# One load for two, a release by VectorE, and a split last store in a streaming multiply-add kernel

## The chip, the cores and the metric

The kernel runs on one core of a Trainium2 chip, with the other cores idle. The metric is the device time of one execution in microseconds (us). Each run below also has a profile of one execution, and all executions told of here were marked as in the fast state, with a granted TensorE clock of 1.0. A ratio is the mean time of one kernel's fast runs over that of the other's fast runs of the same rounds on the same chip, so it is not quite the ratio of the medians quoted beside it. The brackets behind a ratio are its 95% interval.

## The reference

```python
B, S, D = 1024, 16, 512          # x, y: [B, S, D] bf16; gamma: [D] bf16
def reference(x, y, gamma):
    return x + gamma * y
```

Seen flat, x and y have 16384 rows of 512 elements, 16.78 MB each. The output is as large, so the kernel moves 50.33 MB.

## The kernel before

Each of the 128 partitions holds 128 rows. The kernel loads y and x, multiplies and adds in place on VectorE, and stores from y's buffer. A partition's rows form three blocks of 4, 60 and 64 rows, each contiguous in DRAM. SyncE issues the loads in one DMA queue (q1 in the profile) and ScalarE issues gamma and the stores in another (q10). All transfers run on the same 16 DMA engines: the two queues' shares of them sum to 98.7%, and at the handover q10's first packets begin one by one as q1's last ones end, from 79.25 to 79.66 us. The trace records them in packets, the pieces that one engine moves one after the other: a load of 64 rows shows as 128 packets of 64 KB, one for each partition, in waves of 16 (the last wave of the changed kernel's loads begins from 77.08 to 77.62), so 8 on every engine.

```python
BLOCKS = [4, 60, 64]
PIECES = [12, 52, 56, 8]          # the pieces that VectorE works on
SP = [
    ('y', 0, 4), ('y', 4, 64),
    ('x', 0, 4, 0), ('x', 4, 64, 4),
    ('y', 64, 128),
    ('x', 64, 120, 12), ('x', 120, 128, 68),   # from row, to row, place in x's buffer
]
ACT = [('g',), ('s', 4, 64), ('s', 0, 4), ('s', 64, 128)]   # gamma, then stores
# ... (how the first loads are held and moved ahead)
RELEASE = ('x', 64, 120, 12)
DVE = [('m', 0), ('m', 1), ('a', 1), ('a', 0), ('m', 2), ('m', 3), ('a', 2), ('a', 3)]
# 'm': y = y * gamma for a piece, 'a': y = x + y for a piece
# ...
    # TensorE waits for the 56-row load of x and lets the stores go
    _take(s_load[RELEASE], 16, nc.tensor)
    nc.tensor.sem_inc(s_go, 1)
    nc.tensor.sem_inc(s_rel, 1)
```

ScalarE waits for `s_go` before its first store. The rows of that store are summed long before, at 58.6 us, so the wait holds the stores back until the loads are nearly through. The last 64 rows of x reuse the part of x's buffer that the first sum frees.

Of the kernel before, what the change touches and what calls it, by code (L numbers as in the profile page):

```python
# [14 lines left out]
    ('x', 0, 4, 0),  # L15
    ('x', 4, 64, 4),
    ('y', 64, 128),
    ('x', 64, 120, 12),
    ('x', 120, 128, 68),
]  # L20
ACT = [('g',), ('s', 4, 64), ('s', 0, 4), ('s', 64, 128)]

EARLY = (2, 0)

HOLD, AHEAD = ('y', 0, 4), (2, 0)

RELEASE = ('x', 64, 120, 12)

DVE = [('m', 0), ('m', 1), ('a', 1), ('a', 0), ('m', 2), ('m', 3), ('a', 2), ('a', 3)]
MULT, ADD = mybir.AluOpType.mult, mybir.AluOpType.add  # L30


def _take(sem, n, eng):


    return eng.wait_ge(sem, n).then_inc(sem, -n)  # L36


def kernel(
# [9 lines left out]
    nc = tc.nc  # L49
# [26 lines left out]
    y_sb = nc.alloc_sbuf_tensor("y_sb", [P, rows, D], dt).ap()  # L76
    x_loads = [w for w in SP + ACT if w[0] == "x"]
    y_loads = [w for w in SP + ACT if w[0] == "y"]
    stores = [w for w in SP + ACT if w[0] == "s"]
    for loads in (x_loads, y_loads, stores):  # L80
# [5 lines left out]
    sem = nc.alloc_semaphore  # L86
    s_gamma, s_ones, s_ps, s_dve = sem("s_gamma"), sem("s_ones"), sem("s_ps"), sem("s_dve")
    s_load = {w: sem("s_" + "_".join(map(str, w[:2]))) for w in x_loads + y_loads}
    s_held = {nc.sync: sem("s_held_sp"), nc.scalar: sem("s_held_act"), nc.vector: sem("s_held_dve")}
    s_add, s_go, s_rel, s_end, s_out = sem("s_add"), sem("s_go"), sem("s_rel"), sem("s_end"), sem("s_out")  # L90
    added = [a for kind, *a in DVE if kind == "a"]
    order = {a[0]: k for k, a in enumerate(added)}

    def meets(a, b, c, d):
        return a < d and c < b
# [4 lines left out]
    def x_at(row):  # L100
        return next(w[3] + row - w[1] for w in x_loads if w[1] <= row < w[2])
# [12 lines left out]
    def ring(eng, what, n_early, n_ahead):  # L114

        known, went = 0, False
        for k, w in enumerate(what):
            kind = w[0]
            if k == n_ahead:
                _take(s_held[eng], 1, eng)  # L120
            need = frees(w) if kind == "x" else pieces_of(w[1], w[2]) + list(w[3:]) if kind == "s" else []
            need = max((order[c] + 1 for c in need), default=0)
            if kind == "s" and not went:
                _take(s_go, 1, eng)
                went = True
            if need > known:
                eng.wait_ge(s_add, need)
                known = need
            if kind == "g":
                i = eng.dma_start(out=gamma_row, in_=gamma.unsqueeze(0)).then_inc(s_gamma, 16)  # L130
            elif kind == "x":
                to = x_sb[:, w[3] : w[3] + w[2] - w[1], :]
                i = eng.dma_start(out=to, in_=rows_of(xf, w[1], w[2])).then_inc(s_load[w], 16)
            elif kind == "y":
                r = slice(w[1], w[2])
                i = eng.dma_start(out=y_sb[:, r, :], in_=rows_of(yf, w[1], w[2])).then_inc(s_load[w], 16)
            else:
                r = slice(w[1], w[2])
                i = eng.dma_start(out=rows_of(of, w[1], w[2]), in_=y_sb[:, r, :]).then_inc(s_out, 16)
            if k < n_early:  # L140
                early.append(i.ins)

    ring(nc.sync, SP, EARLY[0], AHEAD[0])
    ring(nc.scalar, ACT, EARLY[1], AHEAD[1])

# [9 lines left out]
    nc.vector.tensor_copy(out=gamma_sb, in_=gamma_ps).then_inc(s_dve, 1)  # L155
    _take(s_dve, 1, nc.vector)

    _take(s_load[RELEASE], 16, nc.tensor)
    nc.tensor.sem_inc(s_go, 1)
    nc.tensor.sem_inc(s_rel, 1)  # L160

    landed, open_mults = set(), 0

    def need(loads, c):
        for w in loads:
            if w not in landed and meets(starts[c], starts[c + 1], w[1], w[2]):
                if w == RELEASE:
                    _take(s_rel, 1, nc.vector)
                elif w == HOLD:
                    _take(s_held[nc.vector], 1, nc.vector)  # L170
                else:
                    _take(s_load[w], 16, nc.vector)
                landed.add(w)

    for kind, *args in DVE:
        c = args[0]
        yt = y_sb[:, starts[c] : starts[c + 1], :]
        if kind == "m":
            need(y_loads, c)
            g = gamma_sb[:, None, :].to_broadcast([P, PIECES[c], D])  # L180
            nc.vector.tensor_tensor(out=yt, in0=yt, in1=g, op=MULT).then_inc(s_dve, 1)  # L181
            open_mults += 1
        else:
            need(x_loads, c)
            if open_mults:
                _take(s_dve, open_mults, nc.vector)
                open_mults = 0
            at = x_at(starts[c])
            xt = x_sb[:, at : at + PIECES[c], :]
            nc.vector.tensor_tensor(out=yt, in0=xt, in1=yt, op=ADD).then_inc(s_add, 1)  # L190
# [44 lines left out]
```

## Time and profile before

| | before |
|---|---|
| device time, median of 6 runs | 120.03 us (119.81 to 120.50) |
| span of the profiled execution | 118.7 us |
| VectorE busy | 70.0 us, 59% |
| DMA queues q1 and q10, share of 16 engines | 66.0% + 32.7% |
| first store issued | 77.86 us |
| x's last rows landed | 80.0 us |
| last store landed | 118.7 us |

The two DMA shares sum to 98.7%; the prediction works out what follows from that. VectorE is busy for 59% of the span, so what matters in this kernel is whether the DMA engines are ever without a packet, and whether each packet takes its usual time (2.42 us for 64 KB and 2.27 us for 60 KB in these traces). The prediction below looked hard at the first question and hardly at the second.

### The profile page before, as it was taken

How to read it: one execution, taken by the hardware profiler on the slowest of the kernel's cores; microseconds unless marked ns; L12 is line 12 of the kernel's file. 1: busy time of each engine (PE TensorE's matmuls, PEld its weight loads, DVE VectorE, ACT ScalarE, POOL GpSimd, SP SyncE). 2: the span in 40 equal slices, each digit the busy share in tenths (PEclk: the TensorE clock that was granted, in tenths of full speed). 3: DMA queues.
4: the chain of work that ended last, by engine and by line, in shares of the span. 5: the costliest groups of instructions: out<-in, count | busy, mean ns of one | idle time of the engine just before them, and what ended most of it. 6: DMA issues, size and time to landing. Idle time of an engine off the chain costs nothing. (4 is left out here: it accounts for less than half of the span.)

```text
span 118.7 us, 89 instructions
## 1 busy us (share of the span) xinstructions
PE 0.6 (0%) x1; PEld 0.1 (0%) x1; DVE 70.0 (59%) x10; POOL 0.2 (0%) x4
## 2 busy tenths in 40 slices
PE   0001000000000000000000000000000000000000
PEld 0000000000000000000000000000000000000000
DVE  0002000699999299999769999989999910000000
POOL 0000000000000000000000000000000000000000
DMA  9779977999779888988897997897997799988892
GB/s 508 331 332 497 497 331 331 508 414 580 331 331 662 353 353 375 684 353 353 353 618 309 502 425 309 359 635 331 393 600 331 331 403 458 707 353 353 353 596 110
DMA packets 1442, 50.33 MB, mean 424 GB/s; under 512 B 161, under 2 KB 162, under 8 KB 546
## 3 DMA queue, kind: packets, MB, share of 16 engines
q1 hardware_dynamic: 1008, 33.55, 66.0%
q10 hardware_dynamic: 434, 16.78, 32.7%
HBM read 33.56 MB, written 16.78 MB: 424 GB/s over the span
## 5 line engine op out<-in xcount | busy, mean ns | idle before, releaser
L181 DVE TENSOR_TENSOR y_sb<-y_sb,gamma_sb 128x6144 bf16<-128x6144 bf16 (+3 forms) x4 | 34.6, 8689 | 12.3 <-DVEq L36 12.3
L190 DVE TENSOR_TENSOR y_sb<-x_sb,y_sb 128x26624 bf16<-128x26624 bf16 (+3 forms) x4 | 34.6, 8688 | 2.6 <-DVEq L36 2.6
L155 DVE CAST gamma_sb<-gamma_ps 128x512 bf16<-128x512 f32 x1 | 0.7, 692 | 8.6 <-DVEq L36 8.6
L147 DVE MEMSET ones_row<- 1x128 bf16 x1 | 0.2, 165 | 2.0 <-PEq L52 2.0
L153 PE MATMUL gamma_ps<-gamma_row,ones_row 1*128 1x512 bf16 x1 | 0.6, 578 | 10.0 <-PEq L36 10.0
L153 PEld LDWEIGHTS gamma_ps<-gamma_row,ones_row 1*128 1x128 bf16 x1 | 0.1, 99 | 10.0 <-issue 10.0
L219 POOL MEMSET const-bfloat16-1.0<- 128x1 bf16 x1 | 0.1, 102 | 0.0
L219 POOL MEMSET const-uint8-127<- 128x1 uint8 x1 | 0.1, 101 | 0.0
L219 POOL MEMSET const-float32-0.0<- 128x1 f32 x1 | 0.1, 99 | 0.2 <-issue 0.2
L219 POOL MEMSET const-float32-1.0<- 128x1 f32 x1 | 0.1, 98 | 0.0
## 6 DMA issues: line engine op xcount, KB each, us to landing
y_sb<-in_y_dram SPq DMA_DIRECT2D x1, 7680.0 KB, 21.2
x_sb<-in_x_dram SPq DMA_DIRECT2D x1, 7680.0 KB, 37.1
out_dram<-y_sb ACTq DMA_DIRECT2D x1, 7680.0 KB, 20.3
x_sb<-in_x_dram SPq DMA_DIRECT2D x1, 7168.0 KB, 22.2
x_sb<-in_x_dram SPq DMA_DIRECT2D x1, 1024.0 KB, 24.3
y_sb<-in_y_dram SPq DMA_DIRECT2D x1, 512.0 KB, 3.2
x_sb<-in_x_dram SPq DMA_DIRECT2D x1, 512.0 KB, 19.3
out_dram<-y_sb ACTq DMA_DIRECT2D x1, 512.0 KB, 21.1
```

Of the source, the lines that this page charges most:

```text
L147: nc.vector.memset(ones_row, 1.0).then_inc(s_ones, 1)
L153: nc.tensor.matmul(gamma_ps, ones_row, gamma_row, start=True, stop=True).then_inc(s_ps, 1)
L155: nc.vector.tensor_copy(out=gamma_sb, in_=gamma_ps).then_inc(s_dve, 1)
L181: nc.vector.tensor_tensor(out=yt, in0=yt, in1=g, op=MULT).then_inc(s_dve, 1)
L190: nc.vector.tensor_tensor(out=yt, in0=xt, in1=yt, op=ADD).then_inc(s_add, 1)
L219: nc = _bacc.Bacc("TRN2", target_bir_lowering=False, num_devices=1)
```

## The change

The intent was to drop the small load at the end: x's last 64 rows come in one load, the stores are released by an event that falls at about the same time anyway (the end of VectorE's last product), and the last store is split so that the larger part can leave first.

```diff
-    ('x', 64, 120, 12),
-    ('x', 120, 128, 68),
+    ('x', 64, 128, 12),
 ]
-ACT = [('g',), ('s', 4, 64), ('s', 0, 4), ('s', 64, 128)]
+ACT = [('g',), ('s', 4, 64), ('s', 0, 4), ('s', 64, 120), ('s', 120, 128)]
...
-RELEASE = ('x', 64, 120, 12)
-
-DVE = [('m', 0), ('m', 1), ('a', 1), ('a', 0), ('m', 2), ('m', 3), ('a', 2), ('a', 3)]
+DVE = [('m', 0), ('m', 1), ('a', 1), ('a', 0), ('m', 2), ('m', 3), ('go',), ('a', 2), ('a', 3)]
...
-    _take(s_load[RELEASE], 16, nc.tensor)
-    nc.tensor.sem_inc(s_go, 1)
-    nc.tensor.sem_inc(s_rel, 1)
...
+        if kind == "go":
+            _take(s_dve, open_mults, nc.vector)   # the products have ended
+            open_mults = 0
+            nc.vector.sem_inc(s_go, 1)
+            continue
```

More of the change, by code (lines that the diff above doesn't have):

```diff
@@ L89 @@
     s_held = {nc.sync: sem("s_held_sp"), nc.scalar: sem("s_held_act"), nc.vector: sem("s_held_dve")}
-    s_add, s_go, s_rel, s_end, s_out = sem("s_add"), sem("s_go"), sem("s_rel"), sem("s_end"), sem("s_out")
+    s_add, s_go, s_end, s_out = sem("s_add"), sem("s_go"), sem("s_end"), sem("s_out")
     added = [a for kind, *a in DVE if kind == "a"]
@@ L166, in need @@
             if w not in landed and meets(starts[c], starts[c + 1], w[1], w[2]):
-                if w == RELEASE:
-                    _take(s_rel, 1, nc.vector)
-                elif w == HOLD:
+                if w == HOLD:
                     _take(s_held[nc.vector], 1, nc.vector)
```

## The prediction

> **What bounds the kernel now.** I first read the page's busy shares and its DMA queues, because a kernel that multiplies and adds once per element is likely to be bound by its bytes.
>
> ```profile
> PE 0.6 (0%) x1; PEld 0.1 (0%) x1; DVE 70.0 (59%) x10; POOL 0.2 (0%) x4
> ...
> q1 hardware_dynamic: 1008, 33.55, 66.0%
> q10 hardware_dynamic: 434, 16.78, 32.7%
> HBM read 33.56 MB, written 16.78 MB: 424 GB/s over the span
> ```
>
> VectorE works for 59% of the span. The two DMA queues, q1 (all of x and y) and q10 (gamma and the stores), together fill 66.0 + 32.7 = 98.7% of the time of the 16 DMA engines. What is left is 1.3% of 118.7 us, or 1.5 us, and most of it is the start and the final landing. So there is one question: does the change make a hole in the DMA stream, or close one?
>
> Next I asked for windows, in which the last two numbers of a row are the DMA share and the GB/s of packets that began there. A row that starts or ends inside a wave of packets misleads, so I moved the bounds to where one load hands over to the next.
>
> ```profile
> 0.00:0.95 0.95, 0.00 (x0) 0.00 (x0) 0.00 (x0) 0.20 (x4) 1.00 0.00 0
> 0.95:1.40 0.45, 0.00 (x0) 0.00 (x0) 0.00 (x0) 0.00 (x0) 1.00 0.90 146
> ...
> 40.20:59.50 19.30, 0.00 (x0) 0.00 (x0) 17.29 (x2) 0.00 (x0) 1.00 1.00 435
> 59.50:79.24 19.74, 0.00 (x0) 0.00 (x0) 18.38 (x3) 0.00 (x0) 1.00 1.00 423
> 79.24:97.30 18.06, 0.00 (x0) 0.00 (x0) 16.21 (x2) 0.00 (x0) 1.00 1.01 437
> 98.60:118.00 19.40, 0.00 (x0) 0.00 (x0) 0.00 (x0) 0.00 (x0) 1.00 1.00 434
> ```
>
> y's last 64 rows (40.20 to 59.50), the first stores (79.24 to 97.30) and the last store (98.60 to 118.00) all run at 434 to 437 GB/s and a share of 1.00: there are no holes, not even where loads give way to stores. The last 64 rows of x (59.50 to 79.24) run at 423. The share is 1.00 there too, so the engines were busy but moved their packets more slowly: 2.7% of 19.74 us, about 0.5 us by this row.
>
> The timeline gives the order round the handover, and the issue list the times from issue to landing.
>
> ```profile
> 55.31 0.80 SPq L133 DMA_DIRECT2D x_sb<-in_x_dram  x2
> 60.49 17.30 DVE L181 TENSOR_TENSOR y_sb<-y_sb,gamma_sb 128x28672 bf16<-128x28672 bf16 x2 [1.94 <-DVEq L36]
> 77.86 17.96 ACTq L139 DMA_DIRECT2D out_dram<-y_sb  x3
> 78.15 17.29 DVE L190 TENSOR_TENSOR y_sb<-x_sb,y_sb 128x28672 bf16<-128x28672 bf16 x2 [0.36 <-DVEq L36]
> ```
>
> ```profile
> x_sb<-in_x_dram SPq DMA_DIRECT2D x1, 7168.0 KB, 22.2
> x_sb<-in_x_dram SPq DMA_DIRECT2D x1, 1024.0 KB, 24.3
> out_dram<-y_sb ACTq DMA_DIRECT2D x1, 23.2
> ```
>
> The 56-row load of x, issued at 55.31, lands at 55.31 + 22.2 = 77.5. TensorE sees that and releases ScalarE's queue, which issues the first store at 77.86: 0.36 us from landing to issue. Behind the 56 rows the 8-row load (issued at about 55.7) keeps the DMA engines fed until 55.7 + 24.3 = 80.0. Those 2.5 us cover the start of the stores. In the window from 77.80 to 79.24 the trace shows packets of q1 alone; q10's begin right after, so the first store packet came at most 1.4 us after its issue, without a hole. The last store, issued at 95.48, lands 23.2 us later, at 118.7, the end of the span.
>
> [...] Here the first load is issued at 0.00 and no packet starts before 0.95, so I use 1.0 to 1.4 us. [...]
>
> **The change part by part.**
>
> *One load of 64 rows for 56 + 8.* The bytes are equal. An 8 KB packet took 0.309 us: between 77.80 and 79.24, 72 packets filled 96.6% of 16 engines (1.44 x 16 x 0.966 / 72). At 435/16 = 27.2 KB per us it would be 0.301. Each engine has 8 of them, so the merger saves 8 x 0.008 = 0.06 us. It may save more: the 56-row load skips 8 rows in every partition's 64 KB of DRAM, and it is the only load in the slow row above, while y's unbroken 64-row load had 435. If skipping is the cause, up to 0.3 to 0.5 us comes back. One stretch can't show that, so I give it a third of its weight: -0.1 us.
>
> *VectorE releases the stores.* The last product ends at 60.49 + 17.30 = 77.79, 0.3 us after the landing that released them before. The chain behind it has as many steps as the old one (wait, increment, ScalarE's wait, issue), so 0.36 us again: stores are issued at about 78.15, not 77.86, or 0.3 us later. Their first packets are ready 1.0 to 1.4 us on, at 79.15 to 79.55. The load's last packets end between 79.24 and about 79.7, engine by engine, or some 0.3 earlier if the slow row vanishes. So the cover that the 8 rows gave shrinks to about nothing: an engine is either just in time or dry for some 0.1 to 0.3 us. A start on an empty engine is slower too: the first 16 packets (0.95 to 1.40) took 0.90 x 0.45 = 0.40 us each where 4 KB at 27.2 KB per us is 0.15. Only the engine that finishes last counts, and the one whose load ends last is the least likely to run dry. I put this at +0.1 to +0.2 us.
>
> *The last store as 56 + 8 rows.* It gives back the 0.06 us of small packets. The 56-row store needs the sum of those rows, which now waits for all 64 rows of x: start at about 80.1 instead of 78.15, end at 80.1 + 15.1 = 95.2. The sum of the last 8 rows follows without a gap (2.29 us), to 97.4. The stores before keep the engines busy until about 98.6, and 95.2 + 1.4 = 96.6, so 2 us of margin are left where there were 98.6 - (95.48 + 1.4) = 1.7. The 8-row store is needed only 56/64 of 19.4 us after that. Nothing of this reaches the end.
>
> Sum: -0.06 - 0.1 + 0.15 + 0.06 = +0.05 us, which is nothing beside the spread of the three runs (0.2 us).
>
> **The rivals.** *The stream breaks at the handover.* The later release and a cold start cost every engine their whole 0.3 + 0.25 us: 120.6. The late release speaks for it; against it is that data was moving on every engine until 79.24. It would take a start of 2.5 us or more to reach 122.5, and the trace has 1.4 at most. *The slow stretch was the skipping load.* Then the end comes 0.3 to 0.5 us earlier, 119.6 to 119.8, if the stores are ready in time, which the release at 78.15 makes doubtful; the skipping moves into the 56-row store, though the first stores, which do not skip, say nothing of its rate. *VectorE's later sums starve the last stores.* The sum starts 2 us later and would have to end after 97.2 to matter; the time stays 120.1 unless x lands over 2 us late. *A smaller last store lands sooner.* Packets of 8 KB at the end could even out the engines, but each has the same bytes as before: at most 0.2 us, 119.9.
>
> **Range and chances.** All of these lie within 0.5 us of 120.1, and 2% is 2.4 us, four times the largest term. I predict 120.15 us, with 119.7 to 120.6 for 8 in 10, and 0.97 for within 2%. The rest goes mostly to slower, since a hole in the stream can only cost.
>
> **What would show it right or wrong.** Right: the first store is issued at 78.1 to 78.2; the x load lands at 79.6 to 80.0; the DMA share of the handover (about 79 to 80) stays near 1.00, or falls short by less than 0.5 us on any engine; the first sum runs from about 80.1 to 95.2; the two shares still sum to over 98%. The skipping rival is right if the windows of x's last load show 434. I am wrong if q10's first packets come after 80.2, if a hole opens near 98.6 because a store was issued late, or if the final landing takes much longer after the last packet than now.

## The result, and the profile after

The changed kernel took 120.81 us (median of 6, 120.59 to 121.29) against 120.03 us, a ratio of 1.0066 [1.0040, 1.0091]. It is within 2%, but 0.8 us slower, and outside the predicted range.

The page of the changed kernel, busy DMA queues (packets, MB, share of 16 engines):

```profile
q1 hardware_dynamic: 864, 33.55, 65.6%
q10 hardware_dynamic: 578, 16.78, 33.0%
HBM read 33.56 MB, written 16.78 MB: 420 GB/s over the span
```

The shares still sum to 98.6%: the engines did not stand idle. But they moved 420 GB/s instead of 424, so some packets took longer. Windows of the changed kernel with bounds laid between waves of packets show which (the last two numbers of a row are the DMA share and the GB/s of packets that began in it):

```profile
40.30:59.60 19.30, 0.00 (x0) 0.00 (x0) 17.29 (x2) 0.00 (x0) 1.00 1.01 435
59.60:79.50 19.90, 0.00 (x0) 0.00 (x0) 17.29 (x2) 0.00 (x0) 1.00 0.99 422
79.50:82.53 3.03, 0.00 (x0) 0.00 (x0) 2.04 (x1) 0.00 (x0) 1.00 1.01 324
82.53:98.35 15.82, 0.00 (x0) 0.00 (x0) 15.25 (x2) 0.00 (x0) 1.00 1.00 435
```

From 79.50 to 82.53 the engines are full (1.01) and yet move 324 GB/s. This is the wave of the first store packets, one on each engine. The DMA queues of this window, first for the kernel before (79.24 to 81.48), then for the changed one (79.50 to 82.53):

```profile
q10 hardware_dynamic: 16, 0.98, 101.2%
```

```profile
q10 hardware_dynamic: 16, 0.98, 100.9%
```

In both it is 16 packets of q10 and 0.98 MB. Before, 1.012 x 2.24 us gives 2.27 us a packet; after, 1.009 x 3.03 gives 3.06 us. The second and later packets are at full rate again (435). So each engine lost on average 3.06 - 2.27 = 0.8 us on its first store packet, and nothing to speak of after it.

The order of things in the timeline of the changed kernel, and its issues with the time from issue to landing:

```profile
60.87 17.29 DVE L177 TENSOR_TENSOR y_sb<-y_sb,gamma_sb 128x28672 bf16<-128x28672 bf16 x2 [2.10 <-DVEq L33]
78.43 2.51 ACTq L136 DMA_DIRECT2D out_dram<-y_sb  x2
80.49 15.09 DVE L186 TENSOR_TENSOR y_sb<-x_sb,y_sb 128x28672 bf16<-128x28672 bf16 x1 [2.32 <-DVEq L33]
```

```profile
out_dram<-y_sb ACTq DMA_DIRECT2D x1, 7680.0 KB, 20.9
...
x_sb<-in_x_dram SPq DMA_DIRECT2D x1, 24.8
```

VectorE's last product ends at 60.87 + 17.29 = 78.16 and the first store is issued 0.27 us later. The load of x, issued at 55.53, lands at 80.3, and the 60-row store at 78.43 + 20.9 = 99.3, which is 19.0 us after x. Before, it was 77.86 + 20.3 = 98.2, or 18.2 us after x. The issue of two stores at the handover also took 2.51 us of ScalarE's queue in all; of this the second took 2.11 where it took 0.45 before.

This profiled execution (121.29 us) is the slowest of the six. Its y landed 0.37 us later than in the profile before, and that is not part of the change: the loads until then are the same. To compare runs in spite of such differences I use two stretches of the trace: from the landing of y's last rows to the landing of x's last rows ("load stretch"), and from there to the landing of the first two stores, 64 rows in all ("store stretch").

| | load stretch | store stretch |
|---|---|---|
| before | 19.63 | 19.39 |
| changed | 19.61 | 20.24 |

The store stretch is 0.85 us longer. The load stretch of both profiles holds a slow passage of some 0.2 us, which most runs below don't have (19.34 to 19.43).

### The profile page after: what moved, and what is told of

Its sections match the earlier page's. It is cut to its first block, busy times and chain, and to the rows that moved or that the text cites. A ratio compares the mean times of both kernels' runs of the same rounds, so it can differ in the third digit from the quotient of the medians.

```text
span 120.0 us, 86 instructions
## 1 busy us (share of the span) xinstructions
PE 0.6 (0%) x1; PEld 0.1 (0%) x1; DVE 70.0 (58%) x10; POOL 0.2 (0%) x4
## 6 DMA issues: line engine op xcount, KB each, us to landing
out_dram<-y_sb ACTq DMA_DIRECT2D x1, 7680.0 KB, 20.9
```

## The experiments

All were timed over five rounds beside the kernel before, on the chip of their group. Of the 18 kernels all gave right results.

| run (edit) | median us | ratio [95%] | load stretch | store stretch |
|---|---|---|---|---|
| b_split_store_only | 120.01 | 0.9999 [0.9983, 1.0014] | 19.42 | 19.37 |
| c_split_load_dve | 120.08 | 1.0016 [0.9992, 1.0039] | 19.42 | 19.37 |
| d_one_load_one_store | 120.71 | 1.0069 [1.0044, 1.0094] | 19.34 | 20.25 |
| g_go_after_m2 | 121.12 | 1.0093 [1.0077, 1.0109] | 20.30 | 19.43 |
| h_second_store_later | 120.78 | 1.0061 [1.0044, 1.0078] | 19.34 | (one store) |
| i_load_8_56 | 120.78 | 1.0065 [1.0049, 1.0081] | 19.43 | 20.15 |
| j_load_32_32 | 120.69 | 1.0068 [1.0043, 1.0093] | 19.69 | 20.24 |
| f_go_at_landing | 121.86 | 1.0159 [1.0138, 1.0179] | 19.34 | 21.26 |
| k_stores_on_sp | 119.85 | 1.0006 [0.9992, 1.0021] | 19.37 | 19.43 |
| l_stores_on_sp_early | 121.15 | 1.0100 [1.0085, 1.0114] | 20.45 | 19.44 |
| n_load_48_16 | 120.54 | 1.0057 [1.0036, 1.0077] | 19.42 | 20.00 |
| m_x_on_act | 121.19 | 1.0107 [1.0094, 1.0121] | (two queues) | 19.43 |
| p_small_store_first | 120.25 | 1.0027 [1.0014, 1.0040] | 19.34 | 19.63 |
| q_early_load_56_8 | 121.19 | 1.0098 [1.0084, 1.0111] | 20.40 | 19.42 |
| r_early_small_store_first | 121.07 | 1.0095 [1.0081, 1.0110] | 20.29 | 19.45 |
| v_sp_go_after_m2 | 121.10 | 1.0099 [1.0084, 1.0114] | 20.59 | 19.44 |
| w_go_a_little_later | 120.29 | 1.0028 [1.0012, 1.0043] | 19.41 | 19.73 |
| x_go_after_m2_load_56_8 | 120.90 | 1.0077 [1.0061, 1.0093] | 19.73 | 19.43 |

The kernel before was at 119.89 to 119.98 us in all these groups. In what follows the "turn" is the moment at which the engines go from the last load packet to the first store packet. Times of single packets without a line beside them are from the packet records of the kept traces.

The expectations, each recorded before its run, number the theories as they came up: 1 is that the stores come too late, 2 that the 64 KB load packets ahead of them delay their start, 3 that the split of the last store costs the time. The later ones are stated where they first appear. What theories 1, 2 and 4 suppose of the fetching of packets and of descriptors was the author's guess: no trace shows it.

### Which part of the change costs

**The last store's split alone**, on the kernel before:

```diff
-ACT = [('g',), ('s', 4, 64), ('s', 0, 4), ('s', 64, 128)]
+ACT = [('g',), ('s', 4, 64), ('s', 0, 4), ('s', 64, 120), ('s', 120, 128)]
```

> The kernel before with only the last store split into 56 and 8 rows. Theories 1 and 2: ratio 1.000 to 1.001 (8 KB packets of 0.309 us instead of 0.302 cost 0.06 us). Theory 3: ratio 1.004 to 1.008.

The ratio is 0.9999: the split costs nothing that can be measured.

**The release by VectorE alone** (the changed kernel with the two loads of x and the whole last store back):

```diff
-    ('x', 64, 128, 12),
+    ('x', 64, 120, 12),
+    ('x', 120, 128, 68),
```

> The changed kernel with x's last rows loaded as 56 + 8 again and the last store whole, so only the release by VectorE is left of the change. Theory 1 (late release: the stores come to the DMA engines 0.3 to 0.6 us later, so each engine's first store packet starts with nothing fetched ahead and takes 3.0 us instead of 2.27): about +0.6 to +0.8 us on the kernel before, ratio 1.005 to 1.007, first store packets near 3.0 us. Theory 2 (the 64 KB load packets: with eight 8 KB packets last on each engine the store is taken up in time even when it is issued 0.3 us later): ratio 1.000 to 1.002, first store packets 2.27 us. Theory 3 (the split of the last store costs the time): ratio 1.000.

The first store is issued at 78.22, which is 0.36 and 0.49 us later than in the two profiles with the old release (77.86 and 77.73), and the time stays: 1.0016 with an interval that holds 1. The store stretch is 19.37 us. So this later release alone was harmless behind 8 KB packets. Theory 1 as I first stated it, that the stores simply come too late, fails here. ScalarE's second issue took 1.57 us in this run too, without harm, so that long issue is not itself the loss.

**The single load and the release, with the last store whole:**

```diff
-ACT = [('g',), ('s', 4, 64), ('s', 0, 4), ('s', 64, 120), ('s', 120, 128)]
+ACT = [('g',), ('s', 4, 64), ('s', 0, 4), ('s', 64, 128)]
```

> The changed kernel with the last store whole. Theories 1 and 2: no gain on the changed kernel, ratio to before 1.005 to 1.008, first store packets still near 3.0 us. Theory 3 (the split store): back to 1.000 to 1.002.

1.0069, as the changed kernel. The DMA queues over the first store packets, for c_split_load_dve (79.02 to 81.35) and then for this run (79.02 to 81.30):

```profile
q10 hardware_dynamic: 16, 0.98, 98.8%
```

```profile
q10 hardware_dynamic: 16, 0.98, 114.0%
```

That is 0.988 x 2.33 = 2.30 us a packet with 56 + 8 rows and 1.14 x 2.28 = 2.60 us with 64. The loss comes with the single load, and only its place is open. In this trace the first store packets take from 2.31 us, on the engines that finished their loads first, to 3.12 us, on those that finished last. The loss grows with the time that a load still ran after the first store packet began anywhere (79.03): 0.04 us where the load had ended by then, 0.44 to 0.48 where it ran 0.16 to 0.20 us longer, 0.78 to 0.85 where it ran 0.39 us longer. The store stretch is 0.88 us longer than in c_split_load_dve (20.25 against 19.37). That is near the largest of these losses and not near their average, 2.60 - 2.27 = 0.33 us: here the engine that finished last set the end.

### Too late or too early

**An earlier release**, after the product of 56 rows and before that of 8:

```diff
-('m', 2), ('m', 3), ('go',), ('a', 2), ('a', 3)]
+('m', 2), ('go',), ('m', 3), ('a', 2), ('a', 3)]
```

> The changed kernel, but VectorE releases the stores after its 56-row product, before the 8-row one: first store issued at about 75.9 us instead of 78.4, before the last load packet of each engine starts (77.1 to 77.6). Theories 1 and 2: the stores are fetched in time, first store packets 2.27 us, ratio 0.998 to 1.001; the load of x lands up to 2.3 us later because a store packet goes in between on each engine, which the sums can afford. Theory 3: ratio still 1.004 to 1.008.

All three theories missed. The run was slower than the changed kernel, 1.0093, and the loss had moved. Windows of this run over the last two waves of load packets and the first of store packets:

```profile
74.13:76.57 2.44, 0.00 (x0) 0.00 (x0) 2.20 (x2) 0.00 (x0) 1.00 0.99 430
76.57:79.64 3.07, 0.00 (x0) 0.00 (x0) 1.77 (x1) 0.00 (x0) 1.00 1.04 342
79.64:81.91 2.27, 0.00 (x0) 0.00 (x0) 0.79 (x1) 0.00 (x0) 1.00 1.02 433
```

Now the last load packets are slow (342 GB/s, 1.04 x 3.07 = 3.2 us each instead of 2.42), and the first store packets run at their usual rate. The first store was issued at 76.07, so that it came to the engines while those load packets were under way: at about 76.93 as an estimate, with the 0.86 us from issue to first packet that f_go_at_landing shows below. So in this run, where the stores came some 2.7 us before the first store packets began (79.64), the loss is in the load packet. In the changed kernel, where they came just before its end (issued at 78.43, so at about 79.29 by the same estimate, with load packets ending from 79.51 to 80.04), the last load packets kept their 2.42 us and the first store packets paid. ScalarE's issue of the two stores took 4.65 us here in all, against 2.51 in the changed kernel and 0.84 in the kernel before.

**A release after the landing of x**, so that no load is in flight:

```diff
         if kind == "go":
+            need(x_loads, 2)
             _take(s_dve, open_mults, nc.vector)
```

> The changed kernel with VectorE releasing the stores only after the landing of x's last load, so that no load is in flight when they come. Theory 1 in its simple form (the loss is the start of a store on an engine with nothing in flight): an open gap of 1 us or more and then still about 3.0 us for the first store packets; ratio 1.015 to 1.02. Theory 5 (the loss needs a load in flight): a gap of 1.0 to 1.5 us between the last load packet and the first store packet, and first store packets of 2.27 to 2.5 us; ratio 1.010 to 1.015.

Windows of this run across the turn:

```profile
79.00:81.04 2.04, 0.00 (x0) 0.00 (x0) 0.89 (x1) 0.00 (x0) 1.00 0.00 0
81.04:83.36 2.32, 0.00 (x0) 0.00 (x0) 2.32 (x1) 0.00 (x0) 1.00 1.00 424
```

No packet begins for 2.04 us (the last load packet ends 1.6 us before 81.04), but the first store packets then take 1.00 x 2.32 us, or 2.33 us by their records: here the stores that began on empty engines paid 0.06 us a packet, not 0.8. The issue at 80.18 and the first packet at 81.04 also give the way of a store to the engines: 0.86 us to the first, about 1.0 to the last, where the prediction took 1.0 to 1.4. The ratio of 1.0159 lies on theory 1's side of the expectations and the packets on theory 5's; the hole was longer than I had set.

**A release some 0.3 us later than in the changed kernel:**

```diff
             open_mults = 0
+            nc.vector.memset(ones_row, 1.0).then_inc(s_dve, 1)
+            _take(s_dve, 1, nc.vector)
             nc.vector.sem_inc(s_go, 1)
```

> The changed kernel with one small memset and its wait between VectorE's last product and the release: the first store is issued some 0.3 us later than in the changed kernel. In the run with release at the landing the first store packets started 0.86 to 1.0 us after the issue, so here they arrive when most engines have just finished their loads. Too early (theory 12): first store packets of 2.3 to 2.5 us, a gap of 0 to 0.5 us before them, ratio 1.001 to 1.004, so faster than the changed kernel. Too late (theory 1): slower than the changed kernel by the 0.3 us, ratio 1.008 to 1.010.

It was the sharpest test: does delaying the stores make the kernel faster? It does, 1.0028 against 1.0066 and 1.0069 for the single load with the earlier release. The intervals just touch, and the runs were made on different chips, but the slowest execution here (120.54 us) is faster than the fastest of those (120.55 and 120.59). Timeline of this run, then its windows from the end of the loads on:

```profile
78.77 1.25 ACTq L136 DMA_DIRECT2D out_dram<-y_sb  x2
```

```profile
79.25:79.63 0.38, 0.00 (x0) 0.00 (x0) 0.00 (x0) 0.00 (x0) 1.00 0.02 0
79.63:81.95 2.32, 0.00 (x0) 0.00 (x0) 1.69 (x1) 0.00 (x0) 1.00 1.01 424
```

78.77 + 0.86 = 79.63, the time of the first store packet. Most engines stand empty for up to 0.4 us before it, which is what the prediction feared, and it is still cheaper than being in time: the first store packets take 2.34 us on average (2.52 on the one engine whose load ended only then). The store stretch is 19.73 us, against 20.24 in the changed kernel. Behind a single load of 64 KB packets the stores of the changed kernel come too early, not too late.

### What the loads and stores at the turn look like

**Only one store at the handover:**

```diff
-ACT = [('g',), ('s', 4, 64), ('s', 0, 4), ('s', 64, 120), ('s', 120, 128)]
+ACT = [('g',), ('s', 4, 64), ('s', 64, 120), ('s', 0, 4), ('s', 120, 128)]
```

> The changed kernel with the 4-row store issued third, at 95 us or later, so that only one store is issued at the handover. In the changed kernel ScalarE's second issue there takes 2.11 us instead of 0.45. Theory 4 (the second issue close behind the first holds up the descriptors of both, and that stretches the first store packets): back to a ratio of 1.000 to 1.002 and first store packets of 2.27 us. Theory 5 (a store that comes to an engine while one of its 64 KB load packets is in flight loses about 0.8 us there, whatever follows): ratio still 1.005 to 1.008, first store packets near 3.0 us.

1.0061, first store packets up to 3.11 us. The second store has no part in the loss of this run.

**The 8 rows first, the 56 rows last:**

```diff
-    ('x', 64, 128, 12),
+    ('x', 64, 72, 12),
+    ('x', 72, 128, 20),
```

> The changed kernel with x's last rows in two loads again, but the 8 rows first and the 56 rows last, so that the packets in flight when the stores come are of 56 KB, and two loads are queued. Theory 5 (size of the load packet in flight at the arrival of the stores): ratio 1.005 to 1.008, first store packets near 3.0 us. Theory 6 (two loads in the queue instead of one is what helps, whatever their size): ratio 1.000 to 1.002.

1.0065, first store packets of 2.31 to 3.19 us. Two loads in the queue don't help as such: with the same two sizes in the other order (c_split_load_dve) the loss is gone, 1.0016. So what counts here is which packets stand next to the turn.

**Packets of 32 KB and of 16 KB:** loads of 32 and 32 rows, and of 48 and 16 rows, otherwise the same edit.

> The changed kernel with x's last rows as two loads of 32 rows: packets of 32 KB (1.21 us) in flight at the arrival of the stores. Theory 5: a loss between none and that of the 64 KB packets, on the engines whose last packet is still in flight; first store packets of 2.3 to 2.9 us, ratio 1.001 to 1.006. Theory 6: ratio 1.000 to 1.002 and first store packets of 2.27 us on every engine.

> The changed kernel with x's last rows loaded as 48 and 16 rows, so that packets of 16 KB (0.6 us) are in flight when the stores come, where 8 KB packets lost nothing and 32 KB packets lost 0.8 us. Theory 5 (size of the packet in flight): first store packets between 2.27 and 3.0 us on some engines, ratio 1.001 to 1.006; a ratio of 1.000 or 1.007 puts the limit on one side of 16 KB.

With 32 KB the loss is whole: 1.0068, and 3.07 us a packet on average. My "in between" was wrong: the loss does not shrink with the packet. With 16 KB it is split by engine: 4 of the 16 first store packets took 2.27 us and the others 2.6 to 3.15, for a ratio of 1.0057 and a store stretch of 20.00 us, against 19.37 in c_split_load_dve. With 8 KB packets and the same release (c_split_load_dve) no engine lost more than 0.07 us. So for a store that came at the last moment 8 KB load packets were small enough (1.0016), and 16 KB ones were not (1.0057).

**Small store packets behind the turn:**

```diff
-('s', 4, 64), ('s', 0, 4), ('s', 64, 120), ('s', 120, 128)]
+('s', 0, 4), ('s', 4, 64), ('s', 64, 120), ('s', 120, 128)]
```

> The changed kernel with the 4-row store ahead of the 60-row one, so that the first eight store packets of each engine are of 4 KB. Theory 9 (the loss needs large packets on both sides of the turn): ratio 0.999 to 1.002. Theory 10 (what counts is the load packet in flight when a store arrives): the same loss of about 0.8 us on each engine, on the first 4 KB packets or on the first 60 KB one, ratio 1.005 to 1.008.

Between the two theories: 1.0027. 7 of the 16 engines show a slow 4 KB packet, 0.49 us over its time at most; the rest lost little. Small packets behind the turn helped, but less than small ones ahead of it: the store stretch is 19.63 us, against 19.37 in c_split_load_dve.

### One queue or two

**All stores behind the loads in q1**, released as in the changed kernel:

```diff
     ('x', 64, 128, 12),
+    ('s', 4, 64), ('s', 0, 4), ('s', 64, 120), ('s', 120, 128),
 ]
-ACT = [('g',), ('s', 4, 64), ('s', 0, 4), ('s', 64, 120), ('s', 120, 128)]
+ACT = [('g',)]
```

> The changed kernel with all stores issued by SyncE, behind the loads in the same queue q1; release by VectorE at the end of its last product as in the changed kernel. Theory 7 (the 0.8 us are lost where an engine takes up the other queue while a large packet is in flight): no loss, first store packets of 2.27 to 2.35 us, ratio 0.999 to 1.003. Theory 8 (the loss is in the turn from loads to stores behind a large packet, whatever the queue): first store packets still near 3.0 us, ratio 1.005 to 1.008.

Timeline and windows of this run:

```profile
78.00 0.82 SPq L137 DMA_DIRECT2D out_dram<-y_sb  x2
```

```profile
76.37:78.85 2.48, 0.00 (x0) 0.00 (x0) 1.38 (x1) 0.00 (x0) 1.00 0.98 423
78.85:81.17 2.32, 0.00 (x0) 0.00 (x0) 1.34 (x1) 0.00 (x0) 1.00 0.99 424
```

The first store is issued 1.69 us before x lands, as in d_one_load_one_store (1.64 us), and yet the loss is gone: 1.0006, store stretch 19.43 us, first store packets of 0.99 x 2.32 = 2.3 us, and two issues in 0.82 us. The run also shows that the loss is not simply paid when some engines read while others write: the first store packets began at 78.86, while load packets ran on other engines until 79.39. It looked like theory 7, that an engine loses when it takes up another queue. The runs that follow refute that.

**The same queue, released at 59 us** (the product list becomes `('go',), ('m', 2), ('m', 3)`):

> The same with the release before the product of the last 64 rows, at about 59 us, so that the stores stand in q1 behind the load of x some 20 us before their turn. Theory 7: first store packets 2.27 us, ratio 0.997 to 1.001. Theory 8: if only the turn matters and not when the store arrives, near 3.0 us and ratio 1.005 to 1.008. Either way x lands at the time it does in the changed kernel, about 79.8 to 80.3, because one queue keeps its order.

Windows of this run over the last two load waves and the first of stores:

```profile
74.06:76.48 2.42, 0.00 (x0) 0.00 (x0) 2.42 (x2) 0.00 (x0) 1.00 1.00 433
76.48:80.16 3.68, 0.00 (x0) 0.00 (x0) 1.52 (x1) 0.00 (x0) 1.00 1.01 285
80.16:82.42 2.26, 0.00 (x0) 0.00 (x0) 1.15 (x1) 0.00 (x0) 1.00 1.01 435
```

Both theories failed. With the stores waiting in the same queue for over 17 us before the last wave, the last load packets take 1.005 x 3.68 = 3.7 us instead of 2.42, a loss of 1.28 us on each engine, and x lands late. The queue kept its order: 285 GB/s over 3.68 us is the 1.05 MB of 16 load packets, so no data of a store had begun to move before 80.16, although the first store was issued at 58.79. **Released at 76 us** in the same queue (the edit of g_go_after_m2 on k_stores_on_sp):

> All stores in q1 behind one load of 64 rows, released after the 56-row product: issued at about 76 us, so that they arrive at about 77, while each engine's last load packet is in flight. Theory 10: that packet takes 0.8 to 1.4 us longer, ratio 1.006 to 1.011. If in one queue only a long stay costs: first store and last load packets at their usual times, ratio 0.999 to 1.002.

It is slow as well: 1.0099, load stretch 20.59 us. The last load packets take 3.3 us on average, a loss of 0.9 us; the rest of the longer stretch lies before them in this profile. So in one queue too the stores cost when they came well ahead of the turn; of these three releases in q1 only that at the last moment (issue at 78.00, 1.0006) was free.

**The last load of x in q10, with the stores behind it, released at 59 us:**

```diff
-    ('x', 64, 128, 12),
 ]
-ACT = [('g',), ('s', 4, 64), ('s', 0, 4), ('s', 64, 120), ('s', 120, 128)]
+ACT = [('g',), ('x', 64, 128, 12), ('s', 4, 64), ('s', 0, 4), ('s', 64, 120), ('s', 120, 128)]
...
-('m', 2), ('m', 3), ('go',), ('a', 2), ('a', 3)]
+('go',), ('m', 2), ('m', 3), ('a', 2), ('a', 3)]
```

> The last load of x issued by ScalarE in q10, with all stores behind it in the same queue, released at about 59 us; so the handover from q1 to q10 is now from load to load at 56 to 60 us and the one from load to store stays in one queue. Theory 7: a load packet of y or x between 56 and 63 us takes about 0.8 us longer on every engine, and the first store packets take 2.27 us; ratio 1.004 to 1.008. Theory 8: no long load packet there, first store packets near 3.0 us.

Windows of this run over the handover from q1 to q10, load to load, and over the last wave of loads:

```profile
54.56:66.70 12.14, 0.00 (x0) 0.00 (x0) 7.77 (x3) 0.00 (x0) 1.00 1.01 437
...
76.30:80.10 3.80, 0.00 (x0) 0.00 (x0) 3.80 (x2) 0.00 (x0) 1.00 1.00 276
```

Going from one queue to the other between large load packets cost nothing here (437 GB/s). Going from load to store within one queue cost 1.4 us (3.80 us a packet instead of 2.42). Theory 7 is out as the general cause, and of the causes tried what remains is the direction, from load to store. A turn from store to load was not tried.

### Do small packets protect a store that comes early?

**Stores in q1 at 59 us behind 56 and 8 rows; the same behind 64 rows with the 4-row store first:**

> All stores in q1 and released at 59 us as in the run that lost 1.3 us, but with x's last rows as 56 and 8 rows. Theory 10: with 8 KB packets ahead of the turn nothing, or at most a packet's time (0.3 us), is lost: ratio 0.998 to 1.002. Theory 11 (a store that stands in the queue ahead of its turn costs 1.3 us, whatever the size of the load packets; the kernel before is saved by its late release): ratio 1.008 to 1.012, spread over the 8 KB packets or on the last of 56 KB.

> As the run that lost 1.3 us (one load of 64 rows, stores in q1 released at 59 us), with the 4-row store first. Theory 9: ratio 0.998 to 1.002. Theories 10 and 11: the last load packet of each engine still takes 3.5 to 3.8 us, ratio 1.008 to 1.012.

Neither helps: 1.0098 and 1.0095. In the first, the 8 KB load packets themselves are slow. A window of that run:

```profile
77.00:80.00 3.00, 0.00 (x0) 0.00 (x0) 2.85 (x2) 0.00 (x0) 1.00 0.98 259
```

Theory 11 holds: a store that waits in the loads' queue for some 17 us cost about 1.0 to 1.4 us at the turn with 64 and 8 KB packets ahead of it, and with 60 and 4 KB packets behind it.

**Stores in q10 at 76 us behind 56 and 8 rows** (the edit of g_go_after_m2 with the two loads):

> The run with the release after the 56-row product (stores in q10, issued at about 76 us, ratio 1.009), with x's last rows as 56 and 8 rows. If 8 KB packets protect as such: ratio 1.000 to 1.002. If they only protect a store that comes late among them, as in one queue: the 8 KB packets (or the last of 56 KB) take about 0.8 us longer in sum on each engine, ratio 1.006 to 1.011.

The ratio says that they don't protect here either: 1.0077. The trace explains it only in part. A window of it at the turn:

```profile
78.00:79.00 1.00, 0.00 (x0) 0.00 (x0) 0.85 (x2) 0.00 (x0) 1.00 1.02 344
```

The load stretch is 0.3 us longer than usual, but this profiled execution also lost some 0.4 us in the first 2 us of its loads, which has nothing to do with the turn. The other five executions have no trace, so how they lost their 0.7 to 1.1 us stays open.

## Why the prediction was wrong

- **What bounds the kernel: right.** The engines' share stayed at 98.6%, and all that VectorE lost (the sum starting at 80.49 instead of 78.15) opened no hole in the stream. The sum ended at 80.49 + 15.09 = 95.58, inside the margin that the prediction had worked out, and no hole opened near 98.6 (a share of 1.00 from 98.35 to 116.50). The first store (78.43) and x's landing (80.3) fell outside the times that the prediction had named, but by no more than the 0.37 us that y landed late; d_one_load_one_store had 78.16 and 79.8.
- **The time of the release: right in mechanism.** Product end to issue took 0.27 us where I had set 0.36. I had set the way from the issue to the engines too long: f_go_at_landing shows 0.86 to 1.0 us, and the 1.4 that I read in the kernel before held a wait behind load packets that were still running.
- **"An engine is either just in time or dry for some 0.1 to 0.3 us": the step that failed.** I put the term at +0.1 to +0.2 us and assumed that a store which is in time is free. No engine ran dry, yet the term measured 0.8 us (3.06 against 2.27 us for the first store packet, averaged over the engines). I had looked for holes in the stream and not for slow packets in a full one. The cold start that I feared cost 0.06 us (f_go_at_landing), and standing dry for up to 0.4 us was the better choice (w_go_a_little_later, 1.0028 against 1.0066).
- **"A hole in the stream can only cost": wrong as a rule.** The release at 78.4 is not late but early: some 0.3 us later was faster. What the 8 KB packets gave the kernel before was not only cover, as I read it. They also made the last-moment arrival of the stores free: c_split_load_dve and d_one_load_one_store differ in nothing but the load, and only the second loses (1.0016 against 1.0069).
- **The merger of the loads, 0.06 us and perhaps 0.1 more: half right.** Undisturbed load stretches are 19.42 us with 56 + 8 rows and mostly 19.34 with 64, or 0.08 us. The skipping load was not the cause of the slow row: the unbroken load had 422 GB/s in the changed kernel's profile, and with 56 + 8 rows the stretch was 19.42 in two other runs. The slow passage comes and goes by execution, and against those two runs it is 0.2 us (19.63 in the kernel before), not the 0.5 that the row suggested.
- **The split of the last store, +0.06 us:** too small to be seen, 0.9999 [0.9983, 1.0014]. The 0.2 us of the rival with a smaller last store were a guess, not worked out from the trace.
- **The rival "the stream breaks at the handover"** named the right place, with a size of up to 0.55 us, but the wrong causes (lateness and a cold start), so that its 120.6 came near the measured 120.81 is luck.

What is shown: the loss belongs to the turn from loads to stores. It falls on the last load packets when the stores come well ahead (g_go_after_m2, 3.2 us instead of 2.42), and on the first store packet when they come just before the loads end (the changed kernel, 3.06 us instead of 2.27). It did not need two queues (l_stores_on_sp_early, 1.0100), two stores (h_second_store_later, 1.0061) or one load (i_load_8_56, 1.0065); and stores that came after the last load packet hardly paid it (f_go_at_landing, 2.33 us a packet). Where stores came about 2 us or more ahead of the turn, every run was slower (1.0077 to 1.0107), though in x_go_after_m2_load_56_8 the trace accounts for only a part. Where they came at the last moment, 8 KB load packets (c_split_load_dve, 1.0016) or a single queue (one run, k_stores_on_sp, 1.0006 against 1.0066 for the same release with two queues) avoided it. At a release at 76 us the choice of queue did not help: 1.0099 in one and 1.0093 in two. What happens inside a DMA engine at the turn is not shown: the records give a packet's start and duration, and nothing within it. Nor is it shown why one queue was safe at the last moment and two queues were not.

No version beat the kernel before. The best is k_stores_on_sp, with 119.85 us against 119.89 for the kernel before in its rounds, which is the same.

## What to carry to other kernels

Where a stream of loads turns into a stream of stores, look at the rate of each wave of packets across the turn, not only at the share: here the share was 1.01 while the rate fell to 324 GB/s. Try first not to queue stores early behind large loads (1.0093 to 1.0107 here), but to let them reach the engines as the last load packets end, behind small packets (1.0016) or in the same queue (1.0006), and measure a slightly later release (1.0028) before an earlier one (1.0093). If a small transfer at the end of a tuned kernel's loads looks like mere filler, test its removal alone: here the store stretch was 19.37 us with it and 20.25 without it.
